# Attention before two wide layers: small softmax steps move from GpSimd to VectorE, raw weights get other places, and products on a tile of ones are added

## The chip, the cores and the metric

The kernel runs on one core of one Trainium2 chip. The metric is the device time of one execution in microseconds (us). The engines are named as in the profile: PE (TensorE, with PEld for its weight loads), DVE (VectorE), ACT (ScalarE), POOL (GpSimd) and SP (the queue that issues the DMAs).

## The reference

An attention with two kinds of mask feeds a layer with relu squared, and that feeds a layer with a rational activation. There are 4 batches of 8 heads, 576 positions and 64 numbers a head.

```python
# attention: B, H, S, D = 4, 8, 576, 64; heads 0-3 local, heads 4-7 strided
scores = q @ k.T / sqrt(D)
mask_local = (rel >= 0) & (rel < 32)
mask_strided = (rel >= 0) & (pos[None, :] % 32 == pos[:, None] % 32)
scores = where(mask, scores, -1e9); scores -= max(scores)
attn = exp(scores); attn = attn / (sum(attn) + 1e-09)
x = attn @ v                               # -> 2304 tokens x 512
# layer 1 (2304 x 512, 512 x 2048, 2048 x 512)
h = maximum(x @ w_in, 0); x = (h * h) @ w_out
# layer 2, the same sizes
h = x @ w_in2
P = a0 + a1*h + a2*h**2 + a3*h**3; Q = 1 + |b0|*|h| + |b1|*h**2
out = (P / (Q + 1e-6)) @ w_out2
```

## The kernel before, in words

**Attention.** Two heads and a third of the positions make a group; there are 48, and masked blocks are never computed. A group passes through these steps: scores on PE with the mask added by a product (L288, L296), row maxima on DVE (L307, tile `sm`), the maxima times -1/8 on POOL (L308), `exp` with row sums on ACT (L320), sums plus 1e-9 on POOL (L328), reciprocals on DVE (L329), weights times reciprocals on POOL (L331), transposes on PE (L338) with a copy by DVE or ACT (L344, L346), the values' products on PE (L354), and a split of the result into a high part on ACT (L379) and a low part on DVE (L380), both stored in the layers' input tiles.

**First loop.** The first 14 groups go through `at_slot`, slots 0 to 13, with the later steps of a group some slots behind its scores. In a slot the order is scores (every second slot), maximum, values of an earlier group, transposes of another, `exp`, output, normalization. The other 34 groups are spread over the token blocks of layer 1 by `at_piece`.

**Layers.** Both run over 6 blocks of 384 tokens and, in a block, 16 slices of 128 hidden units. For layer 1 a step is one slice: 12 products into `h` (L457), relu on ACT (L467), square (L469 in block 0 on ACT, L471 later on DVE), a split into `gh` and `gl` (L474, L475), and, two steps later, 12 products into `acc` (L497). Every product is made of three, with high and low parts.

**Weights.** The weights arrive as 64-bit numbers in halves of a slice, 32 halves for each layer. `load_w` (L189) brings a half as a raw tile; `to_f32` makes 32-bit numbers of it with one ACT operation (L201) and three on DVE (L202, L203, L204); `split_w` writes the high part by a cast (L220 on POOL, every fourth on ACT, L218) and the low part (L221, on POOL after the first four). For layer 1 this happens while block 0 runs, two halves a step (`feed_w`). A raw half of layer 1 lies either in a place that will hold finished weights later, as `h12`, or in a ring of three staging buffers (`None`). The list `homes` gives the place of each half in the order of use, counted from 0; a place can be loaded again only when the half before in it was used up. The halves of layer 2 are spilled to DRAM during blocks 1 to 4.

**Order.** A planner orders the instructions of each engine by its own estimates and frees buffers by them, except those passed to `keep_in_program_order`, as PE's in the first groups (`pin`), the `warm_up` products, and most of layer 2. Waits hold up whatever stands behind them on that engine, SP too. The `ps` pool has seven PSUM banks; `wps`, the tile of `warm_up`, takes one of them until its last use.

Of the kernel before, what the change touches and what calls it, by code (L numbers as in the profile page):

```python
# [14 lines left out]
ALU = mybir.AluOpType  # L15
# [11 lines left out]
NF = DFF // P  # L27
# [129 lines left out]
def moe_kernel(ctx, tc, qk, vp, w1, w2, a, b, masks, eye, out):  # L157
    nc = tc.nc
# [54 lines left out]
    def split_w(wh, wl, wf):  # L213

        halves[0] += 1
        n = halves[0]
        if n % 4 == 0:
            nc.scalar.copy(wh, wf)  # L218
        else:
            nc.gpsimd.tensor_scalar(wh, wf, 1.0, 0.0, ALU.mult, ALU.add)  # L220
        (nc.vector if n <= 4 else nc.gpsimd).tensor_tensor(wl, wf, wh.bitcast(F32), ALU.subtract)  # L221
# [14 lines left out]
    def lags(n):  # L236

        return (3, 4) if n < FIRST else (2, 3)
# [29 lines left out]
    def at_scores(n):  # L268

        g = groups[n]  # L270
        nn, late = 2 * g.nt, n >= LATE
        two = []
        for m in range(2):
            ps = psum.tile([P, 512], F32, tag="ps", name=f"ps_s{groups[n + m].name}")
            sc = ps[: g.nq, : nn * g.nk].rearrange("p (h t k) -> p h t k", h=2, t=g.nt)
            flat = ps[: g.nq, : nn * g.nk]
            s3 = flat.rearrange("p (a k) -> p a k", k=g.nk)
            if g.local and g.i == 0:
                mask = cst[:QL, None, C_L0 : C_L0 + 2 * KL].to_broadcast([QL, 2, 2 * KL])
                to = flat.rearrange("p (h k) -> p h k", h=2)  # L280
            else:
                c0 = C_L1 if g.local else C_S7 if g.nr == 7 else C_S4
                mask = cst[: g.nq, None, c0 : c0 + g.nk].to_broadcast([g.nq, nn, g.nk])
                to = s3
            two.append((sc, s3, to, mask))
        if not late:
            for sc, s3, to, mask in two:
                pin(n, nc.tensor.matmul(to, cst[: g.nq, C_ID : C_ID + g.nq], mask, start=True, stop=False))  # L288
        for h in range(2):
            for t in range(g.nt):  # L290
                q0 = h * g.qn + t * g.nq
                k0 = 2 * g.qn + h * g.kn + g.k_starts()[t]
                end = late or (h == 1 and t == g.nt - 1)
                for m in range(2):
                    x = st[n + m]["qk"]
                    mm = nc.tensor.matmul(two[m][0][:, h, t, :], x[:, q0 : q0 + g.nq], x[:, k0 : k0 + g.nk], start=late, stop=end)  # L296
                    pin(n, mm)
        for m, (sc, s3, to, mask) in enumerate(two):
            st[n + m].update(ps=s3, to=to, mask=mask, nn=nn)

    def at_max(n):
        g, s = groups[n], st[n]
        nn = s["nn"]
        if n >= LATE:
            nc.vector.tensor_tensor(s["to"], s["to"], s["mask"], ALU.add)
        sm = s["sm"] = apool.tile([P, 16], F32, tag="sm", name=f"sm{g.name}", bufs=6)
        nc.vector.tensor_reduce(sm[: g.nq, 0:nn], s["ps"], AX.X, ALU.max)  # L307
        nc.gpsimd.tensor_scalar(sm[: g.nq, 4 : 4 + nn], sm[: g.nq, 0:nn], -1.0 / 8.0, 0.0, ALU.mult, ALU.add)  # L308

    def at_exp(n):  # L310
        g, s = groups[n], st[n]
        sm, nn = s["sm"], s["nn"]
        if n < FIRST:
            ea = wpool.tile([P, 1024], F32, tag=f"wl{NF - 1 - n % PLACES}", name=f"ea{g.name}")
            e, s["at"] = ea[:, :512], ea[:, 512:]
        else:
            e = apool.tile([P, 512], F32, tag="e", name=f"e{g.name}", bufs=3)
        s["e"] = e[: g.nq, : nn * g.nk].rearrange("p (a k) -> p a k", k=g.nk)
        for i in range(nn):
            nc.scalar.activation(  # L320
                s["e"][:, i, :], s["ps"][:, i, :], AF.Exp,
                bias=sm[: g.nq, 4 + i : 5 + i], scale=1.0 / 8.0, accum_out=sm[: g.nq, 8 + i : 9 + i],
            )

    def at_norm(n):
        g, s = groups[n], st[n]
        sm, nn = s["sm"], s["nn"]
        nc.gpsimd.tensor_scalar(sm[: g.nq, 8 : 8 + nn], sm[: g.nq, 8 : 8 + nn], 1.0, 1e-9, ALU.mult, ALU.add)  # L328
        nc.vector.reciprocal(sm[: g.nq, 12 : 12 + nn], sm[: g.nq, 8 : 8 + nn])  # L329
        r = sm[: g.nq, 12 : 12 + nn, None].to_broadcast([g.nq, nn, g.nk])  # L330
        nc.gpsimd.tensor_tensor(s["e"], s["e"], r, ALU.mult)  # L331

    def at_transpose(n):
        g, s = groups[n], st[n]
        nn = s["nn"]
        ps = psum.tile([P, 512], F32, tag="ps", name=f"ps_t{g.name}")
        for i in range(nn):
            mm = nc.tensor.transpose(ps[: g.nk, i * g.nq : (i + 1) * g.nq], s["e"][:, i, :], ident[: g.nq, : g.nq])  # L338
            if i == 0:
                pin(n, mm)  # L340
        if "at" not in s:
            s["at"] = apool.tile([P, 512], F32, tag="at", name=f"at{g.name}")
        if n < WARM and n % 2 == 0:
            nc.vector.tensor_copy(s["at"][: g.nk, : nn * g.nq], ps[: g.nk, : nn * g.nq])  # L344
        else:
            nc.scalar.copy(s["at"][: g.nk, : nn * g.nq], ps[: g.nk, : nn * g.nq])  # L346

    def at_values(n):
        g, s = groups[n], st[n]
        ps = psum.tile([P, 512], F32, tag="ps", name=f"ps_v{g.name}")  # L350
        for t in range(g.nt):
            for h in range(2):
                i = h * g.nt + t
                mm = nc.tensor.matmul(  # L354
                    ps[h * D : (h + 1) * D, t * g.nq : (t + 1) * g.nq], s["v"][: g.nk, t, h, :],
                    s["at"][: g.nk, i * g.nq : (i + 1) * g.nq], start=True, stop=True,
                )
                if t == 0 and h == 0:
                    pin(n, mm)
        s["o"] = ps  # L360

    def at_out(n):
        g, s = groups[n], st.pop(n)
        ps = s["o"]
        for j, t0, ar in g.pieces():
            xh, xl = x_block(j)
            if g.local:
                views = [z[:, g.hp, t0 : t0 + 2 * QL] for z in (xh, xl)]
                src = ps[:, : 2 * QL]
            else:  # L370
                a0, na = ar
                views = [
                    z[:, g.hp, t0 : t0 + na * STRIDE]
                    .rearrange("p (a r) -> p a r", r=STRIDE)[:, :, g.r0 : g.r0 + g.nt * g.nr]
                    .rearrange("p a (t r) -> p a t r", t=g.nt)
                    for z in (xh, xl)
                ]
                src = ps[:, : g.qn].rearrange("p (t a r) -> p a t r", t=g.nt, r=g.nr)[:, a0 : a0 + na]
            nc.scalar.copy(views[0], src)  # L379
            nc.vector.tensor_tensor(views[1], src, views[0].bitcast(F32), ALU.subtract)  # L380
# [7 lines left out]
    def load_groups(n):  # L388
        while loaded[0] < min(2 * AHEAD_PAIRS, n):
            load_qk(loaded[0] // 2)  # L390
            load_v(loaded[0] // 2)
            loaded[0] += 2

    def at_slot(n):

        load_groups(n + 4)
        if n % 2 == 0:
            at_scores(n)
        at_max(n)
        if n == 2:  # L400
            warm_up(2)
        for m in range(max(0, n - 4), n):
            if n - m == lags(m)[1]:
                at_values(m)
        for m in range(max(0, n - 4), n):
            if n - m == lags(m)[0]:
                at_transpose(m)
        at_exp(n)
        for m in range(max(0, n - 4), n):
            if n - m == lags(m)[1]:  # L410
                at_out(m)
        at_norm(n)
# [101 lines left out]
    def warm_up(n):  # L514
        for _ in range(n):
            tc.keep_in_program_order(nc.tensor.matmul(wps, warm[:, :P], warm, start=True, stop=True))
# [11 lines left out]
    def load_co():  # L528
# [9 lines left out]
    homes = [  # L538
        ("h8", 0), ("h9", 0), ("h15", 1), ("h14", 3), ("h13", 5), ("h12", 7), ("h11", 9), ("l11", 9), ("h10", 11), ("l10", 10), ("l9", 11), ("l8", 12),
        ("l15", 13), ("l14", 14), ("l13", 15), ("l12", 16),  # L540
    ]
    homes += [(c + str(f), 0) for f in (12, 13, 14, 15, 14, 15) for c in "hl"] + [(None, 0)] * 4
    raws = []

    def load_raw(done):
# [23 lines left out]
    while slot < last[0] + 5:  # L569
        at_slot(slot)  # L570
        slot += 1
        load_raw(fed[0])
        if slot > 9:
            feed_w(1)
# [173 lines left out]
```

## Time and profile before

| | us |
|---|---|
| median of 3 runs | 929.36 |
| lowest and highest | 928.68, 929.71 |
| the profiled execution, its own time | 929.01 |
| its span from first to last instruction | 927.2 |
| PE busy, DVE busy, POOL busy, ACT busy | 899.6, 674.2, 599.1, 548.1 |

The span is what the traced rows cover; 1.8 us of the profiled execution lie around it. Busy times overlap, and an average over the span hides that the stages have different limits, so the rows below go by stretches.

### The profile page before, as it was taken

How to read it: one execution, taken by the hardware profiler on the slowest of the kernel's cores; microseconds unless marked ns; L12 is line 12 of the kernel's file. 1: busy time of each engine (PE TensorE's matmuls, PEld its weight loads, DVE VectorE, ACT ScalarE, POOL GpSimd, SP SyncE). 2: the span in 40 equal slices, each digit the busy share in tenths (PEclk: the TensorE clock that was granted, in tenths of full speed). 3: DMA queues.
4: the chain of work that ended last, by engine and by line, in shares of the span. 5: the costliest groups of instructions: out<-in, count | busy, mean ns of one | idle time of the engine just before them, and what ended most of it. 6: DMA issues, size and time to landing. Idle time of an engine off the chain costs nothing.

```text
span 927.2 us, 14645 instructions
## 1 busy us (share of the span) xinstructions
PE 899.6 (97%) x5232; PEld 825.7 (89%) x5232; DVE 674.2 (73%) x792; ACT 548.1 (59%) x1392; POOL 599.1 (65%) x643
## 2 busy tenths in 40 slices
PE   7799889999999999999999999999999999999998
PEld 4698789998998899999999999899999899899896
DVE  3887774645554554635312689999999999999997
ACT  5785564445444444433324577676776777777774
POOL 3676664554554545544333488888888888888885
PEclk9799899999999999999999999999999999999999
DMA  7863235444444543442377620010010100100000
GB/s 282 316 231 121 92 109 177 160 144 155 131 147 140 174 121 122 162 138 78 123 254 253 218 70 9 18 43 10 23 37 10 51 19 1 43 1 1 35 1 34
DMA packets 40104, 98.55 MB, mean 106 GB/s; under 512 B 4704, under 2 KB 11616, under 8 KB 40032
## 3 DMA queue, kind: packets, MB, share of 16 engines
q1 hardware_dynamic: 40032, 97.62, 31.5%
q8 instruction: 41, 0.67, 0.3%
q14 instruction: 31, 0.25, 0.1%
HBM read 71.39 MB, written 26.21 MB: 105 GB/s over the span
## 4 chain that ended last, share of the span: by engine, by line
DVE 44%; PE 43%; POOL 4%; ACT 4%; DMA 3%; issue 2%; POOLq 0%; SPq 0%; DVEq 0%; ACTq 0%
DVE rq L624 24%; PE h L457 20%; PE acc L497 17%; DVE p L626 9%; DVE rq L635 7%; PE ps_s L296 2%; PE ps_v L354 2%; POOL wl L221 2%; PE ps_t L338 2%; ACT e L320 1%; DVE wraw L204 1%; DMA qk<-in_qk 1%; DMA wraw<-in_w 1%; DVE bits L203 1%; ACT w L201 1%
## 5 line engine op out<-in xcount | busy, mean ns | idle before, releaser
L457 PE MATMUL h<-xh,wh 128*128 128x384 f32 x768 | 264.8, 345 | 3.8 <-ACT r L467 2.3
L457 PE MATMUL h<-xh,wl 128*128 128x384 f32 x768 | 259.6, 338 | 0.0
L457 PE MATMUL h<-xl,wh 128*128 128x384 f32 x768 | 259.1, 337 | 0.0
L624 DVE RECIPROCAL rq<-w 128x384 f32<-128x384 f32 x96 | 243.9, 2541 | 17.3 <-POOL w L622 17.3
L457 PEld LDWEIGHTS h<-xh,wh 128*128 128x128 f32 x768 | 145.8, 190 | 12.0 <-issue 2.6
L457 PEld LDWEIGHTS h<-xl,wh 128*128 128x128 f32 x768 | 145.8, 190 | 3.8
L457 PEld LDWEIGHTS h<-xh,wl 128*128 128x128 f32 x768 | 145.4, 189 | 0.0
L643 POOL TENSOR_TENSOR gl<-rq,gh 128x384 fp32r<-128x384 f32 x96 | 114.7, 1195 | 40.1 <-ACT gh L642 40.1
L475 POOL TENSOR_TENSOR gl<-r,gh 128x384 fp32r<-128x384 f32 x75 | 76.1, 1015 | 88.4 <-ACT gh L474 73.1
L497 PE MATMUL acc<-gh,wl 128*128 128x384 f32 x384 | 129.5, 337 | 2.2 <-POOL wl L221 2.2
L497 PE MATMUL acc<-gh,wh 128*128 128x384 f32 x384 | 129.3, 337 | 1.3 <-ACT wh L218 0.9
L497 PE MATMUL acc<-gl,wh 128*128 128x384 f32 x384 | 128.5, 335 | 0.0
L622 POOL TENSOR_TENSOR w<-w,sq 128x384 f32<-128x384 f32 x96 | 97.8, 1019 | 46.7 <-ACT sq L619 46.7
L623 POOL TENSOR_TENSOR p<-p,hs 128x384 f32<-128x384 f32 x96 | 115.0, 1198 | 0.0
L657 PE MATMUL acc<-wh,gl 128*128 128x512 f32 x288 | 114.0, 396 | 0.3 <-POOL gl L643 0.3
L657 PE MATMUL acc<-wl,gh 128*128 128x512 f32 x288 | 113.7, 395 | 0.0
L657 PE MATMUL acc<-wh,gh 128*128 128x512 f32 x288 | 112.1, 389 | 0.5 <-ACT gh L642 0.5
L642 ACT CAST gh<-rq 128x384 fp32r<-128x384 f32 x96 | 49.4, 515 | 106.5 <-DVE rq L635 106.5
L471 DVE TENSOR_TENSOR r<-r 128x384 f32<-128x384 f32 x75 | 51.7, 689 | 81.9 <-ACT r L467 81.5
L626 DVE SCALAR_TENSOR_TENSOR p<-p,co,hs 128x384 f32<-128x384 f32 x96 | 100.0, 1042 | 0.0
L467 ACT ACTIVATE r<-h 128x384 f32<-128x384 f32 x91 | 44.9, 493 | 91.7 <-PE h L457 84.1
L474 ACT CAST gh<-r 128x384 fp32r<-128x384 f32 x91 | 46.9, 515 | 64.9 <-DVE r L471 64.4
(77 smaller groups left out, 1577.7 us busy)
## 6 DMA issues: line engine op xcount, KB each, us to landing
wraw<-in_w SPq DMA_DIRECT2D x64, 512.0 KB, 4.3
w_scratch<-sph SPq DMA_DIRECT2D x32, 256.0 KB, 4.1
w_scratch<-spl SPq DMA_DIRECT2D x32, 256.0 KB, 3.3
wh<-w_scratch SPq DMA_DIRECT2D x16, 512.0 KB, 3.6
wl<-w_scratch SPq DMA_DIRECT2D x16, 512.0 KB, 4.6
v<-in_vp SPq DMA_DIRECT2D x24, 256.0 KB, 4.2
qk<-in_qk SPq DMA_DIRECT2D x12, 416.0 KB, 4.1
x_scratch<-x SPq DMA_DIRECT2D x24, 192.0 KB, 2.5
```

The lines of the kernel that those rows point to most:

```text
L457: nc.tensor.matmul(ps[:, :TB], w[:, c], x[:, kk, :], start=(kk == 0 and i == 0), stop=(kk == KT - 1 and i == 2))
L471: nc.vector.tensor_tensor(h, h, h, ALU.mult)
L475: low = lambda: (nc.vector if psum_h or j == 0 else nc.gpsimd).tensor_tensor(gl, h, gh.bitcast(F32), ALU.subtract)
L497: nc.tensor.matmul(acc[j][e][:, :TB], w[:, c], g, start=(f == 0 and i == 0), stop=(f == NF - 1 and i == 2))
L622: keep(nc.gpsimd.tensor_tensor(w, w, sq, ALU.add))
L623: keep(nc.gpsimd.tensor_tensor(p1, p1, hs, ALU.mult))
L624: keep(nc.vector.reciprocal(rq, w))
L626: keep(nc.vector.scalar_tensor_tensor(p1, p1, a1, hs, ALU.add, ALU.mult))
L635: keep(nc.vector.scalar_tensor_tensor(rq, p1, a0, rq, ALU.add, ALU.mult))
L642: keep(nc.scalar.copy(gh, rq))
L643: keep(nc.gpsimd.tensor_tensor(gl, rq, gh.bitcast(F32), ALU.subtract))
L657: nc.tensor.matmul(p, g[:, t * P : (t + 1) * P], w[:, c], start=(f == 0 and i == 0), stop=(f == NF - 1 and i == 2))
```

## The change

Four things change; everything else stays. All 32 high parts of layer 1's weights are cast on POOL (eight of them were on ACT). The two small operations on `sm`, L308 and L328, go from POOL to DVE in all 48 groups. In slots 4 to 13 of the first loop two products on the tile of ones are issued, as in slot 2, ahead of the values' products. And the raw halves 16 to 27 of layer 1 get other places, in another order, three of them in the staging ring.

```diff
 def split_w(wh, wl, wf):
-        if n % 4 == 0:
+        if n % 4 == 0 and n > 2 * NF:
             nc.scalar.copy(wh, wf)
         else:
             nc.gpsimd.tensor_scalar(wh, wf, 1.0, 0.0, ALU.mult, ALU.add)
 def at_max(n):
-        nc.gpsimd.tensor_scalar(sm[: g.nq, 4 : 4 + nn], sm[: g.nq, 0:nn], -1.0 / 8.0, 0.0, ALU.mult, ALU.add)
+        nc.vector.tensor_scalar(sm[: g.nq, 4 : 4 + nn], sm[: g.nq, 0:nn], -1.0 / 8.0, 0.0, ALU.mult, ALU.add)
 def at_norm(n):
-        nc.gpsimd.tensor_scalar(sm[: g.nq, 8 : 8 + nn], sm[: g.nq, 8 : 8 + nn], 1.0, 1e-9, ALU.mult, ALU.add)
+        nc.vector.tensor_scalar(sm[: g.nq, 8 : 8 + nn], sm[: g.nq, 8 : 8 + nn], 1.0, 1e-9, ALU.mult, ALU.add)
 def at_slot(n):
         if n == 2:
             warm_up(2)
+        if n > 3:
+            warm_up(2)
 homes = [
         ("h8", 0), ("h9", 0), ("h15", 1), ("h14", 3), ("h13", 5), ("h12", 7), ("h11", 9), ("l11", 9), ("h10", 11), ("l10", 10), ("l9", 11), ("l8", 12),
         ("l15", 13), ("l14", 14), ("l13", 15), ("l12", 16),
 ]
-    homes += [(c + str(f), 0) for f in (12, 13, 14, 15, 14, 15) for c in "hl"] + [(None, 0)] * 4
+    homes += [(x, 0) for x in ("h12", "h13", "h14", "h15", "l15", "l14", "l13", None, None, None, "h15", "l15")] + [(None, 0)] * 4
```

The second number of a pair in `homes` is the slot from which the place may be used.

## Rows read from the trace of the kernel before

**Rows 1.** Windows: us, busy PE, PEld, DVE, ACT, POOL; PEclk, DMA, GB/s.

```profile
12.00:42.20 30.20, 22.48 (x206) 16.14 (x207) 21.86 (x59) 23.85 (x116) 18.79 (x39) 0.81 0.87 307
42.20:80.50 38.30, 38.28 (x257) 35.28 (x255) 33.56 (x64) 27.98 (x79) 27.50 (x35) 0.97 0.57 193
80.50:122.00 41.50, 33.05 (x188) 29.75 (x189) 29.58 (x52) 23.65 (x72) 25.25 (x32) 0.88 0.33 109
122.00:146.00 24.00, 23.16 (x154) 21.67 (x154) 16.16 (x29) 14.87 (x42) 15.07 (x18) 1.00 0.37 118
146.00:520.00 374.00, 371.85 (x2380) 356.02 (x2379) 176.41 (x302) 164.01 (x472) 180.10 (x214) 1.00 0.47 156
520.00:927.20 407.20, 401.82 (x2011) 362.24 (x2009) 393.51 (x284) 289.45 (x599) 331.06 (x300) 1.00 0.09 31
```

**Rows 2.** Chain that ended last, 34 to 51 us: start, us, what.

```profile
34.12 2.07 PE ps_s L296 x16
...
38.17 0.49 issue
...
40.80 0.91 PE ps_v L354 x8
...
42.54 2.93 PE h L457 x12
45.47 0.48 PE ps_v L354 x8
...
46.53 2.09 PE h L457 x12
...
49.05 1.13 PE ps_s L296 x16
```

**Rows 3.** The same chain, 81 to 106 us.

```profile
81.76 4.05 DMA wraw<-in_w
...
101.59 3.85 PE h L457 x12
```

**Rows 4.** Windows about PEclk at half, columns as in group 1.

```profile
30.50:34.00 3.50, 1.74 (x18) 0.98 (x16) 2.79 (x8) 2.48 (x15) 3.34 (x5) 0.99 1.02 347
34.00:44.20 10.20, 8.88 (x58) 7.40 (x59) 8.71 (x20) 8.78 (x39) 6.04 (x13) 0.50 0.98 374
88.60:92.00 3.40, 3.33 (x10) 3.36 (x11) 3.26 (x6) 1.64 (x3) 1.98 (x2) 0.50 0.18 70
98.80:105.60 6.80, 6.32 (x21) 6.20 (x22) 4.06 (x10) 1.86 (x8) 5.87 (x7) 0.50 0.25 80
```

**Rows 5.** Timeline, PE, 10.5 to 12 us: the pair in slot 2.

```profile
10.64 0.60 PE L516 MATMUL wps<-warm 128*128 128x512 bf16 x2
```

**Rows 6.** Groups by line, PE, 12 to 42.2 us: busy, mean, idle before.

```profile
L338 PE MATMUL ps_t<-ident,ea 96*128 96x96 f32 (+2 forms) x44 | 8.0, 313 | 2.2 <-POOL ea L331 2.0 <-ACT xh L379 0.2
L354 PE MATMUL ps_v<-ea,v 128*64 128x96 f32 (+2 forms) x80 | 7.4, 314 | 5.8 <-ACT ea L346 5.6 <-DVE ea L344 0.2
```

**Rows 7.** Waits, 42 to 146 us: total us, times, longest us.

```profile
POOL sm L328 <- ACT e L320: 6.8, 6, 2.0
...
DVE bits L202 <- ACT w L201: 4.4, 2, 3.2
...
DVE xl L380 <- ACT xh L379: 3.5, 3, 3.0
```

**Rows 8.** Groups by line, DVE, 42 to 146 us.

```profile
L475 DVE TENSOR_TENSOR gl<-r,gh 128x384 fp32r<-128x384 f32 x16 | 12.1, 756 | 1.3 <-ACT gh L474 1.1
...
L329 DVE RECIPROCAL sm<-sm 96x4 f32<-96x4 f32 (+2 forms) x11 | 1.9, 172 | 11.9 <-POOL sm L328 11.9
```

**Rows 9.** Groups by line, DVE, 42.2 to 80.5 us.

```profile
L203 DVE SCALAR_TENSOR_TENSOR bits<-wraw,bits 128x512 int32<-128x512 int32 x13 | 9.0, 689 | 0.1
```

**Rows 10.** One line, the DVE part of L475: ns least, median, most.

```profile
L475 DVE TENSOR_TENSOR gl<-r,gh x16: 547/559/1697, 47.7 to 135.5; 128x384 fp32r<-128x384 f32 x16
```

**Rows 11.** One line, the casts on POOL, columns as in group 10.

```profile
L220 POOL TENSOR_SCALAR wh<-wraw x24: 637/657/1052, 24.2 to 133.0; 128x512 fp32r<-128x512 f32 x24
```

## The prediction

> **What bounds the kernel now.** I read the windows by stage first. From 520 us on DVE is busy 393.5 of 407.2 us, and from 146 to 520 PE is busy 371.9 of 374 [rows 1]. Neither stretch is touched where it is limited: the small operations of the groups done there go to a DVE that is busy 176 of 374 us, and layer 2 is as it was. So what is won or lost before 146 us should reach the end whole. Before that, PE's idle time in the three windows from 42.2 to 146 is 103.8 - 94.5 = 9.3 us, nearly all of it after 80.5 [rows 1], and in three stretches the granted clock is at half, 1.2 GHz for 2.4 [rows 4]. In the first loop, 12 to 42.2 us, no engine is full: PE waits 8.0 us ahead of transposes and values, for copies on ACT and normalizations on POOL [rows 6]. Next I followed the chain that ended last through 34 to 51 us and 81 to 106 us [rows 2, 3]; then I read the waits and DVE's groups between 42 and 146 us for the operations that move [rows 7, 8].
>
> **The raw places.** By the list before, half 17 goes to `l12`, which half 15 leaves only when its low part is written. The chain shows just that: a raw transfer begins at 81.76 and lands 4.05 us later [rows 3], and only then can ACT's L201 read it. DVE stood 3.2 us for this ACT operation, the longest of its two such waits [rows 7]. In the new list half 17 goes to `h13`, which half 4 left some 12 halves earlier; `l15`, `l14` and `l13` take halves 20 to 22, each eight halves after the one that leaves; halves 23 to 25 use the ring, and the next two come seven halves after theirs. From 42.2 to 80.5 us DVE made 13 halves, 2.9 us each [rows 9], so that seven are some 20 us against a transfer of 4.05. I take -3.2; bounds 0 (the wait moves) and -4.05 (the whole transfer).
>
> **The products on ones.** Ten pairs. A pair took 0.60 us in slot 2 [rows 5]; most should fall into the 8.0 us in which PE waits anyway [rows 6]. I count two as exposed, those of slots 12 and 13, where scores and not a copy led the chain, at 0.5 each: +1.0. With no cover all ten cost +6.0; with full cover 0. What they may give: in 34.0 to 44.2 the clock was at half after a window in which PE was busy 1.74 of 3.5 us [rows 4], and the chain there has PE steps that appear again at full clock: scores 2.07 against 1.13, values 0.91 against 0.48, 12 products 2.93 against 2.09 [rows 2]. That is -2.2 if the clock stays up, 0 if it falls all the same.
>
> **The second loss of clock.** It falls to half for 3.4 us from 88.6 and 6.8 us from 98.8 [rows 4], after PE starved. With the raw wait gone the first of these should go and the second be shorter. At half clock 12 products of `h` took 3.85 us, against 2.09 at full [rows 2, 3], and DVE stood 3.0 us behind the cast that followed them on ACT [rows 7]. I take 1.8 for that and half of the ten products at 88.6 times 0.15, 0.7: -2.5, between 0 and -3.3.
>
> **L308 and L328 on DVE.** On the chain a stretch of 0.49 us, in which POOL is on a weight cast, stands before L308 [rows 2]; on DVE it follows its maximum at once: -0.4. From 42 to 146 us 20 such operations are added to DVE, which is 88% busy up to 80.5 [rows 1]. The trace has no such operation on DVE; the nearest is L329, as small, 0.172 us [rows 8]. But POOL's neighbours matter. The subtraction L475 takes 0.55 us at best, 0.756 in the mean and 1.70 at most [rows 8, 10], so it is held for up to 1.15 us. If the new ones are held alike, 0.2 in the mean, they cost 0.3 with an allowance for overlap, 20 times: +6.0. Bounds: 0.1 each, +2.0, and 0.54 (below), +10.8. Against it stands L329's idle time, 11.9 us waiting for L328, of which POOL's own wait for ACT explains 6.8 [rows 7, 8]; the other 5.1 is queue and handing over, and goes. Net +0.9. What queues behind such a wait on DVE are L202 to L204 of the next half and L475, for which POOL's L220 and L221 wait, and PE's `acc` products after them; on POOL it was the casts and low parts themselves. In the slots DVE is busy 21.9 of 30.2 us, and 28 times 0.172 is 4.8 us of the 8.3 left [rows 1, 8]; the same hand-overs go, so 0.
>
> The Trainium skill has a rule that would make this dearer (SBUF — State Buffer, section Who interferes with whom): VectorE's one-input `tensor_scalar` in SBUF can take both ports, one pair of which GpSimd shares, and the later of two that meet is fully blocked. The 1.70 us above agrees for an operation with two inputs [rows 10]; no row shows the new form. By it the sum would be the slower rival's, by the measured mean it is +0.9.
>
> **The casts.** Eight casts of 0.66 us go to POOL [rows 11], 5.3 us. POOL is busy 65% from 42.2 to 146, and so has 36 us free [rows 1]; uncovered they would cost up to +5.3. I take 0, since ACT loses as much, and its in-order waits for L204 with it.
>
> **The bank.** `wps` now keeps one of the seven PSUM banks to slot 13. PE's waits in the slots name copies and normalizations, and only 0.2 us the release by L379 [rows 6]. +0.3, between 0 and one values' wait of about 1.0 (5.8 over six).
>
> **Sum.** -3.2 - 2.2 + 1.0 - 2.5 - 0.4 + 0.9 + 0 + 0.3 = -6.1. The profiled execution took 929.0 us, 0.4 under the median of the runs: 922.9, so 923. With the moved operations at their lower bound (2.0 - 5.1 for +0.9) it would be 919; with the second loss of clock as it was and three more pairs exposed (2.5 and 1.5) 926.9.
>
> **Rivals.**
> *PE becomes the only bound up to 146 us.* All idle time there, 9.3, and half of 10.2 us of slow clock, 5.1, go, and the start is 1.6 earlier: 913. For it: PE is full from 42.2 to 80.5. Against it: one step needs two halves, 5.9 us at the pace of that stretch [rows 9], and DVE is 88% busy in it. 10%.
> *The raw wait only moves.* SP issues in order, and halves 28 to 31 now need the ring that 23 to 25 hold; if SP or another place is late, the 3.2 us stay: 926. Against it: five halves lie between a ring buffer's uses. 15%.
> *DVE becomes the bound and it is slower.* A small operation that meets POOL is held for the rest of POOL's. POOL is busy 65%; with half of the longest hold, 0.57, this is 0.37 each, 0.54 with its own 0.17. Twenty in 42 to 146 us and half of the 28 in the slots, 34, cost 18.4. If only half of L329's 11.9 comes back, 6.0, it is +12.4 against gains of 7.3 without this part, so +5.1, 934. It is slower from 0.39 us each on; the mean hold measured, 0.2, 0.37 with its own 0.17, stands just under that. 10%.
> *The change does not do what it says, and nothing moves.* The planner orders DVE and POOL anew, the pairs are exposed or the clock falls all the same, and the raw gain is eaten by waits at other places: +1.0 to +3 on the pairs and 2.2 less, 928 to 930. 10%.
>
> **How the numbers follow.** The forecast has 55%, the others 10, 15, 10 and 10. A measurement of this kernel tells about 0.2%, 1.9 us, from no change. The first three cases are faster by more: 80%; no change 10%; slower 10%. The range leaves out most of the full-PE case and the slower one: 915 to 929; the likeliest case's own is 919 to 926.9.
>
> **What would show it.** Right: PEclk 1.00 from 34 to 44 us; no DMA wait ahead of the eighteenth L201; block 0's accumulators stored some 6 us earlier; PE's idle time between 42 and 146 us under 6; the later stages as long as before. Wrong: small DVE operations on `sm` of 0.5 us and more with POOL busy under them; the clock at half in spite of the pairs; PE waiting in the slots for a bank; ACT waiting for a raw half at another place.

## The result, and the profile after

The changed kernel took 918.75 us (median of four, 917.60 to 922.92) against 929.02 of the kernel before. The ratio is 0.9897, with a 95% interval from 0.9865 to 0.9929: about 10 us faster, 4 us better than the forecast of 923, inside its range of 915 to 929 and just outside the likeliest case's own 919 to 926.9. The profiled execution happens to be the slowest of the four, 922.92 us with a span of 921.1; the other three had granted clocks of 0.993 and 0.994 where this one had 0.991, and took 917.6 to 919.1 us. Its rows therefore stand some 4 us above the median. Lines from 403 on carry numbers two higher than before (L459 for L457, L477 for L475, and so on).

Windows of the changed kernel, columns as in [rows 1], and in the second fence those in which its clock stood at half:

```profile
12.00:42.20 30.20, 24.36 (x210) 15.03 (x214) 23.42 (x75) 21.79 (x104) 12.63 (x15) 0.89 0.79 283
42.20:80.50 38.30, 36.03 (x232) 32.79 (x233) 34.81 (x75) 27.88 (x87) 27.25 (x28) 0.91 0.62 206
80.50:122.00 41.50, 38.46 (x246) 34.79 (x246) 37.23 (x70) 26.47 (x79) 32.44 (x33) 0.96 0.37 123
122.00:146.00 24.00, 23.02 (x153) 21.67 (x152) 17.32 (x32) 12.22 (x37) 14.55 (x15) 1.00 0.44 145
146.00:520.00 374.00, 373.17 (x2390) 357.79 (x2389) 192.07 (x349) 166.05 (x476) 170.44 (x167) 1.00 0.47 156
```

```profile
13.00:19.80 6.80, 6.03 (x35) 3.96 (x38) 2.61 (x14) 4.21 (x24) 3.42 (x4) 0.50 0.94 357
43.70:50.60 6.90, 6.55 (x33) 5.67 (x34) 5.00 (x13) 4.17 (x16) 4.17 (x5) 0.51 0.61 231
98.30:101.80 3.50, 3.50 (x13) 3.50 (x13) 3.44 (x9) 2.91 (x9) 3.50 (x5) 0.51 0.28 90
```

Two things are to be seen against [rows 1, 4]. From 80.5 to 122 PE is busy 38.5 of 41.5 us where it was 33.1, and the slow clock there lasts one stretch of 3.4 us instead of 3.4 and 6.8. But from 42.2 to 80.5 PE is no longer full. The clock is at full from 19.8 to 43.7, where the pairs were to keep it up, and then at half from 43.7 to 50.6, where block 0's first twelve products take 3.89 us for 2.93 [rows 2]. The chain of the changed kernel shows what stands ahead of them (start, us, what):

```profile
37.16 0.60 DVE sm L307
37.75 0.60 DVE bits L203
38.43 0.46 DVE ea L344
38.96 0.26 DVE xl L380
39.31 0.57 DVE wraw L204
39.88 0.60 DVE sm L307
...
42.48 1.14 ACT e L320 x6
...
45.79 3.89 PE h L459 x12
```

Block 0's first twelve products now stand at 45.8 us, where the chain before had them at 42.5 [rows 2], and what leads to them is one DVE operation behind another. The first loop became longer by 3.3 us in this execution; the ground made up lies behind it.

The chain from 80 to 125 us no longer has the raw transfer of [rows 3]; one stands much later:

```profile
79.78 0.61 DVE bits L203
80.41 0.70 DVE wraw L204
81.14 0.68 DVE bits L202
81.81 0.44 issue
82.25 0.70 DVE bits L203
82.97 0.70 DVE wraw L204
...
115.02 5.00 DMA wraw<-in_w
120.11 0.67 ACT w L201
```

Where the raw half came 4 us late, weight steps of DVE follow one another. The transfer at 115.02 is half 30's: its ring buffer is left by half 25, whose low part ends at 115.00. So the raw wait has in part moved to the ring, as the second rival of the prediction had it. What it costs shows in the waits from 42 to 146 us, first of the kernel before, then of the changed one:

```profile
ACT w L201 <- DMA wraw<-in_w: 7.4, 3, 3.3
```

```profile
ACT w L201 <- DMA wraw<-in_w: 4.3, 3, 2.6
DVE bits L202 <- ACT w L201: 0.9, 1, 0.9
```

ACT still waits 4.3 us for raw halves, but DVE waits only 0.9 us behind ACT, where it was 4.4 [rows 7]. And this is how the moved operations fare on DVE, by the groups of its lines from 42 to 146 us (count, busy us, mean ns, idle before):

```profile
L308 DVE TENSOR_SCALAR sm<-sm 96x4 f32<-96x4 f32 (+2 forms) x12 | 4.7, 400 | 0.0
L328 DVE TENSOR_SCALAR sm<-sm 96x4 f32<-96x4 f32 (+2 forms) x12 | 3.0, 253 | 2.6 <-ACT e L320 2.6
L329 DVE RECIPROCAL sm<-sm 96x4 f32<-96x4 f32 (+2 forms) x12 | 2.0, 166 | 0.1
```

L329's idle time of 11.9 us [rows 8] is gone; 2.6 us of waiting for ACT stand at L328 in its place, and the two new lines cost 7.7 us.

### The profile page after: what moved, and what is told of

It is laid out like the page before. It is cut to its first block, busy times and chain, and to the rows that moved or that the text cites. A ratio compares the mean times of both kernels' runs of the same rounds, so it can differ in the third digit from the quotient of the medians.

```text
span 921.1 us, 14748 instructions
## 1 busy us (share of the span) xinstructions
PE 900.4 (98%) x5248; PEld 823.9 (89%) x5252; DVE 697.4 (76%) x888; ACT 544.2 (59%) x1384; POOL 586.0 (64%) x555
## 4 chain that ended last, share of the span: by engine, by line
DVE 47%; PE 44%; ACT 4%; DMA 2%; issue 2%; POOL 1%; SPq 0%; ACTq 0%; POOLq 0%; DVEq 0%
DVE rq L626 24%; PE h L459 20%; PE acc L499 17%; DVE p L628 9%; DVE rq L637 7%; PE ps_v L354 2%; PE ps_t L338 2%; ACT e L320 2%; PE ps_s L296 1%; DVE sm L307 1%; DVE bits L203 1%; DVE wraw L204 1%; DMA x_scratch<-x 1%; PE acc L659 1%; DVE bits L202 1%
## 5 line engine op out<-in xcount | busy, mean ns | idle before, releaser
L459 PE MATMUL h<-xh,wh 128*128 128x384 f32 x768 | 264.4, 344 | 2.3 <-DVE xl L380 0.9
L459 PE MATMUL h<-xh,wl 128*128 128x384 f32 x768 | 259.1, 337 | 0.0
L459 PE MATMUL h<-xl,wh 128*128 128x384 f32 x768 | 258.7, 337 | 0.0
L459 PEld LDWEIGHTS h<-xh,wh 128*128 128x128 f32 x768 | 145.3, 189 | 10.7 <-ACT e L320 1.5
L459 PEld LDWEIGHTS h<-xl,wh 128*128 128x128 f32 x768 | 145.3, 189 | 3.8
L459 PEld LDWEIGHTS h<-xh,wl 128*128 128x128 f32 x768 | 145.1, 189 | 0.0
L477 POOL TENSOR_TENSOR gl<-r,gh 128x384 fp32r<-128x384 f32 x75 | 77.8, 1038 | 80.7 <-ACT gh L476 78.5
L473 DVE TENSOR_TENSOR r<-r 128x384 f32<-128x384 f32 x75 | 56.9, 759 | 80.7 <-ACT r L469 78.7
```

The source lines that it names most:

```text
L459: nc.tensor.matmul(ps[:, :TB], w[:, c], x[:, kk, :], start=(kk == 0 and i == 0), stop=(kk == KT - 1 and i == 2))
L473: nc.vector.tensor_tensor(h, h, h, ALU.mult)
L477: low = lambda: (nc.vector if psum_h or j == 0 else nc.gpsimd).tensor_tensor(gl, h, gh.bitcast(F32), ALU.subtract)
```

## The experiments

All ratios are to the kernel before, run beside each kernel on the same chip. Gains in us below are these ratios times the kernel before. One part alone comes first, then the changed kernel with one part taken back, then parts in pairs.

| kernel | median us | ratio | 95% interval |
|---|---|---|---|
| the changed kernel | 918.75 | 0.9897 | 0.9865 to 0.9929 |
| places alone | 919.91 | 0.9904 | 0.9891 to 0.9917 |
| small operations alone | 926.67 | 0.9968 | 0.9956 to 0.9980 |
| pairs alone | 926.82 | 0.9972 | 0.9963 to 0.9982 |
| casts alone | 929.37 | 0.9994 | 0.9983 to 1.0006 |
| changed, places of before | 926.88 | 0.9971 | 0.9958 to 0.9984 |
| changed, small operations on POOL | 924.29 | 0.9950 | 0.9936 to 0.9963 |
| changed, no pairs | 918.62 | 0.9889 | 0.9872 to 0.9906 |
| changed, casts of before | 920.14 | 0.9902 | 0.9886 to 0.9917 |
| half 17 alone | 924.40 | 0.9955 | 0.9942 to 0.9967 |
| places and casts | 921.13 | 0.9924 | 0.9905 to 0.9942 |
| places and pairs | 925.59 | 0.9961 | 0.9946 to 0.9976 |
| places and small operations | 917.16 | 0.9887 | 0.9866 to 0.9907 |

There is one trace of each kernel, and the traces differ at the start, where no edit has touched anything yet. The first 16 products of the scores take 2.07 us in ten of them and 1.15 in four (places alone, half 17 alone, changed with small operations on POOL, changed with casts of before), so the first row maximum starts at 8.1 to 8.4 us in the ten and at 6.6 to 6.9 in the four. A lead of this kind is named below where it bears on a reading.

**The places alone.**

```diff
-    homes += [(c + str(f), 0) for f in (12, 13, 14, 15, 14, 15) for c in "hl"] + [(None, 0)] * 4
+    homes += [(x, 0) for x in ("h12", "h13", "h14", "h15", "l15", "l14", "l13", None, None, None, "h15", "l15")] + [(None, 0)] * 4
```

> The kernel before with the new raw places alone. My theory, in which the raw wait at 81.8 us and the slow clock behind it are the largest part: 5 to 6 us faster (3.2 for the wait, 2.5 for the clock), with no wait for a raw half ahead of the eighteenth L201 and at most one stretch at half clock after 80 us. The rival, that the wait only moves or that the moved small operations are what gained: 0 to 2 us faster.

8.9 us faster, more than my theory's 5 to 6 and almost all of what the whole change gives. The window from 80.5 to 122 us in this kernel, to be set beside the third line of [rows 1]:

```profile
80.50:122.00 41.50, 37.11 (x244) 33.64 (x245) 36.86 (x67) 28.30 (x84) 32.48 (x38) 1.00 0.39 126
```

PE does 244 products there instead of 188 at a clock that never falls, and DVE is busy 36.9 us instead of 29.6: both had been starved. The early start of this trace has little part in that, since block 0's second slice begins at 46.06 us, against 46.29 in the kernel before.

**Half 17 alone.** One entry of the list of before is replaced.

```diff
     homes += [(c + str(f), 0) for f in (12, 13, 14, 15, 14, 15) for c in "hl"] + [(None, 0)] * 4
+    homes[17] = (None, 0)
```

> The kernel before with one entry of the list of places changed: half 17 goes to the staging ring and not to l12. If the wait for this half and the slow clock behind it are all that the new places take away, it is 7 to 9 us faster than before, as the places alone were (8.9). If the other new places matter as much (halves 24 to 27 came 4 halves after those in their places, now 7 or 8), it is 3 to 5 us faster. If the wait only moves to the next half, 0 to 2.

4.2 us faster, so the first expectation falls and the second holds; of the lead in its trace, 0.7 us are there at block 0's second slice already. The raw wait goes on in this kernel: ACT waits 1.7 us for half 19, whose transfer begins at 78.93, and the chain then shows this:

```profile
98.91 1.54 POOL wl L221
...
100.46 4.55 DMA wraw<-in_w
...
105.04 0.67 ACT w L201
```

This is half 25, whose place `l14` half 21 leaves with its low part at 100.4: the same wait, eight halves later. The other entries of the list carry the other 4.7 us.

**The small operations alone.**

```diff
-        nc.gpsimd.tensor_scalar(sm[: g.nq, 4 : 4 + nn], ...
+        nc.vector.tensor_scalar(sm[: g.nq, 4 : 4 + nn], ...
-        nc.gpsimd.tensor_scalar(sm[: g.nq, 8 : 8 + nn], ...
+        nc.vector.tensor_scalar(sm[: g.nq, 8 : 8 + nn], ...
```

> The kernel before with L308 and L328 on DVE alone. My theory: within 1 us of the kernel before (+0.9 for 20 operations on DVE, -0.4 at the chain's L308). The rival, that DVE is held for the rest of POOL's operations and becomes the bound of the first loop: 3 to 5 us slower, block 0's first product 3 us later or more than 42.2 us. A second rival, that the hand-over it saves is worth more than that: 2 to 4 us faster.

3.0 us faster, the second rival's size. Its trace has both sides. Block 0's first product starts at 44.06 us, 1.8 later than before, and DVE's lines from 42 to 146 us are dearer even than in the changed kernel:

```profile
L308 DVE TENSOR_SCALAR sm<-sm 96x4 f32<-96x4 f32 (+2 forms) x11 | 5.9, 545 | 0.0
L328 DVE TENSOR_SCALAR sm<-sm 96x4 f32<-96x4 f32 (+2 forms) x12 | 4.6, 386 | 3.4 <-ACT e L320 3.4
```

10.5 us of new work, against 8.5 us of L329's waiting (11.9 less 3.4) that go: by DVE's own account a loss of 2.0, and yet the kernel gains. So the gain is not in DVE's sum. It may lie with those that wait for the maxima and the sums, or with what was queued behind the two operations on POOL; neither was measured.

**The pairs alone.**

```diff
         if n == 2:
             warm_up(2)
+        if n > 3:
+            warm_up(2)
```

> The kernel before with the ten pairs on the tile of ones alone. My theory: the clock stays at full from 34 to 44 us, 1 to 1.5 us faster (2.2 less 1.0). The rival, that the pairs are exposed or cost a PSUM bank and the clock falls in any case: 0 to 3 us slower.

2.6 us faster, somewhat more than my theory, but not by its way. The clock does stay up from 34 to 42.8 us, as this window shows, and still block 0's first product comes at 43.48, later than the 42.25 of before:

```profile
34.00:42.80 8.80, 6.04 (x66) 3.90 (x66) 7.36 (x17) 7.26 (x33) 4.78 (x12) 1.00 0.98 362
```

In this window PE, at full clock, is busy only 6.0 of 8.8 us: it waits for others, and a faster PE gains nothing there. What is won lies after the first loop, as the window from 42.2 to 146 us shows, first before, then with the pairs:

```profile
42.20:146.00 103.80, 94.48 (x598) 86.70 (x597) 79.30 (x143) 66.50 (x192) 67.82 (x82) 0.94 0.43 142
```

```profile
42.20:146.00 103.80, 94.58 (x616) 86.05 (x617) 81.83 (x147) 66.81 (x198) 69.29 (x85) 0.97 0.44 146
```

PE is busy for the same time and, by the records, makes 18 more products at a higher clock; from block 0's second slice to its last store it takes 101.8 us for 104.8. Why the clock falls less there is open.

**The casts alone.**

```diff
-        if n % 4 == 0:
+        if n % 4 == 0 and n > 2 * NF:
             nc.scalar.copy(wh, wf)
```

> The kernel before with all 32 casts of layer 1 on POOL alone. My theory: within 1 us of the kernel before, as POOL has 36 us free from 42 to 146. The rival, that POOL's queue delays the low parts for PE: 2 to 5 us slower.

No change that can be told from none, as I had it.

**The changed kernel with one part taken back.** Each undoes one of the four diffs above.

> The changed kernel with the raw places of before. Alone, the places gave 8.9 us, the small operations 3.0, the pairs 2.6 and the casts nothing. If each part earns what it earned alone, this one is 5 to 6 us faster than the kernel before. If all of them work on the same idle time, which the places remove by themselves, it is also some 5 us faster, but taking the places away costs less than 8.9, about 4. If the parts hinder each other, as the start of block 0 at 45.5 us in the changed kernel suggests, it is 0 to 3 us faster.

2.7 us faster than before. Without the places, the three other parts together bring what the small operations or the pairs bring alone, and not the 6.2 of their sum: they hinder each other, or work on the same idle time.

> The changed kernel with L308 and L328 back on POOL. If the small operations on DVE earn their 3 us here too, it is 3 us slower than the changed kernel, 6 to 7 us faster than before. If DVE is held by POOL and by ACT's exponentials in the first loop of the changed kernel (block 0 began 3.3 us later than in the kernel before), it is 2 to 4 us faster than the changed kernel, 12 to 14 us faster than before, with block 0's first product at 42 us or earlier.

4.6 us faster than before, 5.0 slower than the changed kernel. The small operations earn 5.0 here and 3.0 alone, which the intervals do not tell apart. Block 0's first product comes at 41.74 us, 3.8 earlier than in the changed kernel, of which 1.8 are the early start of this trace. So the small operations do lengthen the first loop of the changed kernel, by 2.0 us in these traces, and my suspicion is refuted only as far as the whole time goes.

> The changed kernel without the ten pairs. If they keep up the clock as they did alone, it is 2 to 3 us slower than the changed kernel, 7 us faster than before. If they are exposed, or hold a bank that is missed, now that the small operations are on DVE, it is as fast or up to 3 us faster than the changed kernel, with block 0's first product before 45.5 us.

10.3 us faster than before by its ratio, the same as the changed kernel. In the changed kernel the pairs bring nothing. Without them block 0's first product comes at 44.01 us, ahead of 45.49, as the second expectation has it.

> The changed kernel with every fourth cast of layer 1 back on ACT. If the casts cost nothing on either engine, as alone, it is within 1 us of the changed kernel, 9 to 11 us faster than before. If POOL's queue matters once the raw wait is gone, it is 2 to 4 us faster than the changed kernel.

9.1 us faster: the casts make no difference here either that the intervals can tell.

**Parts in pairs.** Three more kernels, the places with one other part each.

> The new places and the casts on POOL, nothing else. The places alone gave 8.9 us, with casts and pairs 5.1. If the casts hurt, because L308 and L328 stand behind them in POOL's queue once the raw wait is gone: 4 to 6 us faster than before. If the pairs hurt: 8 to 10 us faster.

7.1 us faster, between the two expectations: the interval overlaps that of the places alone, and no loss of 4 us from the casts is seen. A loss of some 2 is not excluded.

> The new places and the ten pairs, nothing else. If the casts hurt the kernel with places, casts and pairs: 9 to 12 us faster than before. If the pairs hurt it: 4 to 6 us faster.

3.6 us faster, and that is 5.3 less than the places alone, with intervals far apart. So it is mostly the pairs that cost the kernel with places, casts and pairs its time. The first product of block 0 comes at 43.39 us, against 40.70 with the places alone (1.3 of the 2.7 are the early start of that trace), and in the window from 80.5 to 122 us PE does less and the clock falls again:

```profile
80.50:122.00 41.50, 36.15 (x232) 32.76 (x231) 36.72 (x65) 27.65 (x82) 30.06 (x36) 0.96 0.35 110
```

> The new places and L308 and L328 on DVE, nothing else. If the small operations earn their 3 us on top of the places: 12 us faster than before. If places and small operations take away the same idle time of block 0: 8 to 10 us faster, no better than the places alone or the changed kernel.

10.5 us faster: as the second expectation has it, no better than the changed kernel as far as intervals tell, and only 1.6 better than the places alone, whose interval it overlaps. Its one trace is the cleanest of all in the stage in question:

```profile
80.50:122.00 41.50, 39.56 (x258) 35.69 (x258) 39.56 (x75) 27.86 (x83) 31.72 (x31) 1.00 0.39 126
```

It has the lowest median of all, and beats the kernel before clearly; the changed kernel it does not beat clear of noise.

**The pairs in the first loop.** Five kernels here differ from another one by the pairs alone. For these, the time from the start of the first row maximum to that of block 0's first product, and the granted clock from 12 to 42.2 us:

| kernel without the pairs | us without | us with | PEclk without | PEclk with |
|---|---|---|---|---|
| before | 34.05 | 35.37 | 0.81 | 0.94 |
| places | 33.80 | 35.20 | 0.84 | 0.94 |
| places and casts | 34.25 | 35.06 | 0.79 | 0.94 |
| places and small operations | 32.37 | 35.00 | 0.90 | 0.89 |
| changed, no pairs | 35.93 | 37.05 | 0.77 | 0.89 |

The pairs raise the clock in four of five, and the first loop is longer in all five, by 0.8 to 2.6 us.

## Why the prediction was right, and where its terms were off

The direction, the range and the main cause, the raw transfers, were right. The sum, -6.1 against some -10, was made of terms that were off on both sides, so that it came as near as it did is in part luck. Of the signs of being right, two came true: the clock at full from 34 to 43.7 us, and the eighteenth L201 without a wait for a transfer. Block 0's last store came 3.8 us earlier and not 6, and PE's idle time from 42 to 146 us was 6.3 us and not under 6. Of the signs of being wrong, three were seen: long DVE operations on `sm`, the clock at half behind the pairs, and ACT waiting for raw halves at another place.

**The raw places and the clock behind them** were mis-sized: -3.2 and -2.5 predicted, -8.9 measured alone. I read the list for half 17, which the chain shows [rows 3], and priced one wait. Halves 24 to 27 came only four halves after those in their places and were late in the same way; in the kernel before this stood behind the slow products of [rows 3], so that the chain ran through PE. Half 17 alone measures 4.2. Of the second loss of clock I counted 2.5 of at most 3.3; with the places alone the clock does not fall at all between 80.5 and 122. That PE's idle time and slow clock go together with the raw wait, which was the rival of a PE that is the only bound, came nearer to it than my term.

**The pairs** were the step that failed: -2.2 and +1.0 predicted. The 2.2 took for granted that a full clock shortens the first loop. The clock did stay up, from 34 to 42.8 us in the kernel with the pairs alone and to 43.7 in the changed one, and the loop became longer all the same, by 0.8 to 2.6 us in five comparisons; the half clock that follows falls on block 0's first products. The changed kernel's clock also fell at 13.0 us. The kernel before has a like stretch, which I did not count:

```profile
16.90:20.30 3.40, 3.40 (x22) 2.28 (x20) 1.53 (x7) 2.02 (x12) 2.17 (x6) 0.50 0.63 229
```

By the whole time, the pairs alone bring 2.6 us; on top of the places they cost 5.3; in the changed kernel they bring nothing. Three answers to one edit cannot be the price of twenty products. The planner makes another order with them: up to 150 us, 176 of the 220 DVE operations of the kernel with the places alone, told apart by kind and tile, can be found in the same sequence in the one with places and pairs; between the changed kernel and that without pairs it is 243 of 262. That fits, but it is an argument and not a test: the bank that `wps` holds was not varied, nor was an order kept fixed. The cause of the three answers stays open.

**The small operations** had the wrong sign in the sum, +0.9 - 0.4 predicted, -3.0 alone. Their price on DVE was right for the changed kernel: 0.3 each predicted, 0.32 measured (7.7 us for 24). With the small operations alone it was 0.46 (10.5 us for 23), above the 0.39 from which the slower rival would have won, and still that kernel gained. The give-back was too small: the waiting there fell by 9.3 us (11.9 at L329 to 2.6 at L328), not by 5.1; that I let ACT's 6.8 stand whole is the likely reason. In the slots I took 0, and there the first loop did become DVE's: 3.3 us later in the changed kernel's trace, 1.8 with the small operations alone. Of these 3.3 the pairs have 1.5 (45.49 against 44.01 without them). In the trace with places and small operations the loop is shorter than with the places alone, 32.4 for 33.8 us from the first row maximum, so it does not hold in every order. This is the mechanism of the slower rival, and it is real; but it was decided by what the later stage gave. That rival's gains without this part are 7.0 by my own terms and not 7.3, which changes nothing.

**The casts** at 0 held as far as the intervals can tell. **The later stages** are not as long as before. From the last store of block 0's results (by the start of its issue 151.0 us in the kernel before, 147.2 in the changed one) to the end it takes 773.9 us, where it took 776.2. In the six traces with the small operations on DVE this stretch is 773.9 to 775.2 us long, in the eight others 775.1 to 776.2, so these operations, which also move in the later groups, probably have a part in it; my prediction had nothing for them there.

**The sum** assumed that terms add. Alone the four parts give 8.9, 3.0, 2.6 and 0.6, 15.1 us; together 9.6 by the ratio. Three of them change the stretch where PE and DVE were idle; once the raw halves come in time, little is left to win there. For the pairs this is not the whole story, since with them the places gain less than alone.

## What to carry to other kernels

When a chain shows one late transfer, follow the list that made it late to its end: the next entries of the same kind hide behind whatever the first delay sets off, here a slow clock that looked like a cause of its own. A higher granted clock in a stretch where PE waits for others need not shorten it. Price parts of a change that work on the same idle stretch as alternatives and not as a sum. And where a planner orders the engines, a part measured alone says little about the same part beside others: take it away from the whole as well.

## What the runs showed of the hardware

A DVE operation of four numbers a row, from SBUF to SBUF, can be held until an operation of POOL has ended. In the changed kernel L308 takes 0.158 us in the median, but 0.998 at most, and L328 up to 1.241. One such meeting, in the timelines of DVE and then of POOL:

```profile
95.28 0.97 DVE L308 TENSOR_SCALAR sm<-sm 96x4 f32<-96x4 f32 x1
```

```profile
94.92 1.31 POOL L221 TENSOR_TENSOR wl<-wraw,wh 128x512 fp32r<-128x512 f32 x1
```

It starts 0.36 us after POOL's subtraction and ends when that has ended, 96.25 and 96.23. In the traces of the six kernels that have L308 and L328 on DVE, 39 of these operations last 0.3 us or more between 42 and 146 us, and each of them ends 20 to 30 ns after an operation of POOL. The Trainium skill (SBUF — State Buffer, section Who interferes with whom) has such a `tensor_scalar` fully blocked by a GpSimd operation that came first; these rows agree. The mean over the stage stayed at 0.40 and 0.25 us, and 0.55 and 0.39 with the small operations alone, so the 0.54 that I gave the slower rival as the price of both was that of L308 alone, in the kernel where it fared worst.
